# A last output stage by seven products, a finer start and a written-out order in an attention and MLP kernel

## The chip, the cores and the metric

One core of a Trainium2 chip. The metric is the device time of one execution in microseconds; lower is better. TensorE is called PE, VectorE DVE, ScalarE ACT, GpSimd POOL and SyncE SP, as in the profile. ACT and SP also issue transfers (queues ACTq and SPq).

## The reference

Causal attention for 4 batches, 12 heads, 448 positions and 64 dimensions per head, all float32, followed by an MLP with squared ReLU:

```python
scores = (q @ k.transpose(0, 1, 3, 2)) / np.sqrt(64)
scores = np.where(mask, -1e9, scores)            # mask: the columns behind the row
attn = softmax(scores)
x = (attn @ v).transpose(0, 2, 1, 3).reshape(1792, 768)
out = np.square(np.maximum(x @ w_in, 0)) @ w_out   # w_in 768 x 2048, w_out 2048 x 768
```

## The kernel before

Two heads make a pair, so there are 24 pairs (6 per batch). The first 12 pairs (batches 0 and 1) feed the first half of the tokens, the other 12 the second half.

**Attention** (`attention`, L341 to L550). A pair's q and k are brought to 64 dimensions x 448 positions per head. Either they are loaded in pieces of 128 bytes, eight transfers per pair (`load_qk`, L356), and transposed on DVE (`transposed`, L403), or they are loaded by rows, four transfers in pieces of 256 bytes (`load_rows`, L378), transposed on PE (`turned_rows`, L389) and copied out by ACT or DVE. `ROWS` says which pairs go by rows: 4 to 9. The scores of a pair (L422) come in seven chunks of 64 query rows; chunk c has 64(c+1) columns, as later columns are masked, so a head has 1792 columns in all. `PLACE` puts the chunks into four PSUM banks, and the first 12 pairs do chunks 6, 5, 0 in one group and 4, 3, 2, 1 in another. For each chunk DVE adds the mask and finds the row's extreme (L435, "mask pass" below), ACT takes the exponential with its sum (L439). When all seven sums are there, DVE forms the reciprocals (L515, L516), POOL or DVE normalises (L448), PE transposes the probabilities in four steps (L462), ACT or DVE copies them out (L318, L470) and PE multiplies by v (L482). Even and odd pairs have a set of buffers each, so the loads of pair 2 into the buffers of pair 0 wait until pair 0's q and k are transposed.

**Two terms.** x, the weights and the hidden values are split into a high and a low part, and a product is three instructions (high by high, high by low, low by high; "step" below), so as to keep float32's precision.

**First half of the tokens.** Plain products: `h_unit` (L679 to L681) and `o_unit` (L1098 to L1100), in four groups of 512 hidden columns.

**Second half of the tokens.** Here each stage is a product of 2 x 2 blocks done with seven block products in place of eight (Winograd's form of Strassen's scheme). `h_pair` makes the hidden values of a group for one of two halves u, `factor` splits them into seven left factors (11, 21, t2, t1, t3, 22, t4), `o_parts` makes the seven right factors from w_out, three loaded and four (s1 to s4) summed by `added_up` with adding transfers from POOL (L742) and copies (L752), and `o_seven` (L986 to L988) multiplies and adds. The groups come in the order `TURNS` = 0, 3, 2, 1. The last, group 1, is the exception: it takes the plain factors (11, 12, 21, 22 on both sides, all eight right factors loaded in two parts from `wo_split`), and `o_last` makes four result blocks with three column blocks d each, four steps x 3 instructions per half u pair, 144 in all. DVE adds each result to its sum (L321), transposes it (L1036), and four transfers of 56 KB store it (L1041). The very last one is stored in another way (`finish`): two halves, each transposed on PE (L1063), copied out and stored (L1078).

**The order.** Every operation is handed to `plan.op` with a rank, the engines that may do it and their costs. `Plan.emit` then runs a list schedule: with planned durations it picks the operation that can start first (by rank between equals), the engine and the buffer, and emits the instructions in the order of their planned starts. `AMENDS` shifts the ranks of stretches of operations. On the chip an engine works through its queue in that order. The order of stages is h of group 0 twice, then for each group the next group's h half 0, its own o stage, the next group's h half 1.

Of the kernel before, what the change touches and what calls it, by code (L numbers as in the profile page):

```python
# [20 lines left out]
class Op:  # L21
    __slots__ = ("rank", "ways", "then", "left", "ready", "take", "drop", "lag", "bias")
# [14 lines left out]
class Plan:  # L37

    LAG = {PE: 0.25, ACT: 0.3, DVE: 0.3, POOL: 0.3, DMA: 0.5, DMA2: 0.5}
    ISSUE = 1.4
    BEGIN, BACKLOG = 1.3, 2.5
    FEW = {PE: 0.0, ACT: 0.5, DVE: 1.0, POOL: 0.0, DMA: 0.0, DMA2: 0.0}
    MANY = {PE: 0.0, ACT: 0.0, DVE: 0.3, POOL: 0.0, DMA: 0.0, DMA2: 0.0}

    def __init__(self):  # L50
        self.ops, self.writer, self.readers = [], {}, {}
        self.pools, self.caps, self.held = {}, {}, {}
        self.bias = self.FEW

# [17 lines left out]
    def op(self, rank, ways, reads=(), writes=(), after=(), take=None, drop=(), clear=(), lag=0.0):  # L72
        o = Op()
        o.rank, o.ways, o.then, o.ready, o.take, o.drop = rank, ways, [], 0.0, take, drop
        o.lag, o.bias = lag, self.bias
# [18 lines left out]
        o.left = len(deps)  # L94
        for d in deps:
            d.then.append(o)
# [3 lines left out]
    def amend(self, table):  # L100
        for first, end, more in table:
            for o in self.ops[first:end]:
                o.rank += more

    def emit(self):
        free = [1.0, 1.9, 3.4, 2.7, 0.7, 0.7]
        ready = [o for o in self.ops if o.left == 0]
        order, port, net = [], 0.0, 0.0
        while ready:
            best = None  # L110
            for o in ready:
                at = o.ready + (self.ISSUE if o.ways[0][0] >= DMA else 0.0)
                if o.take:
                    h, n = o.take[0], len(o.take)
                    if self.held[h.kind] + n > self.caps[h.kind] or len(self.pools[h.pool]) < n:
                        continue
                    at = max(at, sorted(self.pools[h.pool])[n - 1][0])
                at += o.lag
                if o.ways[0][0] >= DMA:
                    at = max(at, net - self.BACKLOG)  # L120

                w = min(
                    (max(free[w[0]], at, port if shared(w) else 0.0) + w[1] + o.bias[w[0]],
# [4 lines left out]
                if best is None or key < best[0]:  # L128
                    best = (key, o, w)
# [61 lines left out]
def kernel(  # L191
# [21 lines left out]
    P = 128  # L213
# [1087 lines left out]
```

## Time and profile before

| | |
|---|---|
| median of 3 runs | 603.56 us (603.54 to 604.6) |
| profiled execution | 606.17 us, span 604.3 us |
| PE busy | 587.0 us, 3766 products and transposes |
| DVE, ACT, POOL busy | 418.8, 361.8, 348.1 us |
| DMA | 120.02 MB, mean 199 GB/s |
| mean granted TensorE clock | 0.999 |

The span runs from the first to the last instruction in the trace; the execution's own time has 1.87 us more around it. Products are pipelined: the duration of one reaches over the start of the next, so the cost of one in a row of many is the distance between two starts.

### The profile page before, as it was taken

What the parts mean: (1) busy time and instruction counts of PE and PEld (TensorE: products, weight loads), DVE (VectorE), ACT (ScalarE), POOL (GpSimd) and SP (SyncE); (2) the same over time, 40 slices, a digit from 0 to 9 for tenths busy, and PEclk for the clock granted to TensorE, in tenths of its full rate; (3) what the DMA queues carried; (4) which work ended last, traced back from release to release, by engine and by line L of the source; (5) the groups of instructions that cost most, each with busy time, mean ns of one, the idle gap of its engine ahead of it and who ended that gap; (6) DMA issues with size and microseconds to landing.
All of it is one profiled execution on the core that took longest, in us unless ns stands there. A gap on an engine that the chain in (4) does not pass through costs nothing.

```text
span 604.3 us, 11456 instructions
## 1 busy us (share of the span) xinstructions
PE 587.0 (97%) x3766; PEld 513.8 (85%) x3766; DVE 418.8 (69%) x951; ACT 361.8 (60%) x889; POOL 348.1 (58%) x460
## 2 busy tenths in 40 slices
PE   3999999999999999999999999999999999999997
PEld 2677777898988998888898889998999899999996
DVE  4997976366985887775677616688782777777454
ACT  3889997665687656577447543367764573752400
POOL 2574673764585844867557754256685566777000
PEclk9999999999999999999999999999999999999999
DMA  9899745979789888987898759869868746771555
GB/s 148 168 204 179 165 103 116 257 232 329 191 208 315 247 238 217 282 232 226 255 242 259 268 189 263 274 188 238 207 152 163 195 116 135 158 177 41 183 92 93
DMA packets 190652, 120.02 MB, mean 199 GB/s; under 512 B 126016, under 2 KB 178560, under 8 KB 190592
## 3 DMA queue, kind: packets, MB, share of 16 engines
q1 hardware_dynamic: 169488, 107.99, 64.8%
q0 software_dynamic: 6912, 9.44, 10.0%
q10 hardware_dynamic: 14192, 1.85, 1.9%
q8 instruction: 30, 0.49, 0.3%
q14 instruction: 30, 0.25, 0.2%
HBM read 80.71 MB, written 38.54 MB: 197 GB/s over the span
## 4 chain that ended last, share of the span: by engine, by line
PE 90%; DMA 4%; ACT 2%; SPq 2%; issue 1%; DVE 0%; ACTq 0%; DVEq 0%
PE ps L1098 7%; PE ps L679 7%; PE ps L1100 6%; PE ps L1099 6%; PE ps L681 6%; PE ps L680 6%; PE ps L482 6%; PE ps L462 6%; PE ps L986 6%; PE ps L988 6%; PE ps L987 6%; PE ps L422 5%; PE ps L860 5%; PE ps L864 5%; PE ps L862 5%; DMA words<-in_moe_w_in_dram 2%
## 5 line engine op out<-in xcount | busy, mean ns | idle before, releaser
L318 ACT ACTIVATE words<-words 128x384 f32<-128x384 f32 (+3 forms) x140 | 79.8, 597 | 27.9 <-DVE words L321 15.3
L448 POOL TENSOR_SCALAR ap<-ap,asm 128x64 f32<-128x64 f32 (+6 forms) x123 | 74.6, 626 | 30.6 <-DVE asm L516 27.7
L435 DVE CUSTOM_DVE_ANT_0 ps<-ps,mask 128x448 f32<-128x448 f32 (+6 forms) x168 | 68.4, 446 | 19.2 <-PE ps L422 12.9
L1098 PE MATMUL ps<-wo,g 128*128 128x384 f32 x224 | 76.8, 343 | 0.0
L1100 PE MATMUL ps<-wo,g 128*128 128x384 f32 x224 | 75.1, 335 | 0.0
L1099 PE MATMUL ps<-wo,g 128*128 128x384 f32 x224 | 75.0, 335 | 0.0
L679 PE MATMUL ps<-x,wi 128*128 128x448 f32 x192 | 74.1, 386 | 0.6 <-ACT aqt L318 0.6
L681 PE MATMUL ps<-x,wi 128*128 128x448 f32 x192 | 70.3, 366 | 0.0
L680 PE MATMUL ps<-x,wi 128*128 128x448 f32 x192 | 70.3, 366 | 0.0
L439 ACT ACTIVATE ap<-ps,mx 128x448 f32<-128x448 f32 (+6 forms) x126 | 59.2, 487 | 15.0 <-DVE mx L435 11.1
L325 POOL TENSOR_TENSOR wi<-words,wi 128x384 fp32r<-128x384 f32 (+1 forms) x44 | 52.6, 1204 | 11.8 <-ACT wi L318 6.6
L860 PE MATMUL ps<-x,wi 128*128 128x448 f32 x156 | 57.3, 367 | 0.3 <-DMA wi<-wi_split 0.3
L318 ACT ACTIVATE r<-ps 128x448 f32<-128x448 f32 x60 | 32.5, 545 | 41.4 <-PE ps L681 17.5
L862 PE MATMUL ps<-x,wi 128*128 128x448 f32 x156 | 57.2, 367 | 0.0
L864 PE MATMUL ps<-x,wi 128*128 128x448 f32 x156 | 57.2, 367 | 0.0
L986 PE MATMUL ps<-g,wi 128*128 128x448 f32 x153 | 56.0, 366 | 0.3 <-DMA wi<-wo_split 0.3
L987 PE MATMUL ps<-g,wi 128*128 128x448 f32 x153 | 56.0, 366 | 0.0
L988 PE MATMUL ps<-g,wi 128*128 128x448 f32 x153 | 56.0, 366 | 0.0
L331 POOL TENSOR_SCALAR wi<-words 128x384 fp32r<-128x384 f32 (+1 forms) x39 | 26.9, 689 | 46.6 <-DVE words L643 23.0
L640 DVE TENSOR_SCALAR words<-words 128x384 int32<-128x384 int32 (+1 forms) x56 | 30.3, 543 | 23.2 <-ACT words L318 23.1
L321 DVE CUSTOM_DVE_ANT_0 words<-words 128x768 uint16<-128x768 uint16 (+1 forms) x56 | 42.3, 755 | 5.8 <-ACT words L318 3.3
L318 ACT ACTIVATE apt<-ps 128x512 f32<-128x512 f32 x65 | 35.6, 611 | 14.5 <-PE ps L462 14.4
(149 smaller groups left out, 1459.9 us busy)
## 6 DMA issues: line engine op xcount, KB each, us to landing
words<-in_moe_w_in_dram SPq DMA_DIRECT2D x24, 512.0 KB, 5.6
words<-in_moe_w_out_dram SPq DMA_DIRECT2D x32, 384.0 KB, 3.7
wo_split<-wo SPq DMA_DIRECT2D x26, 384.0 KB, 4.8
wi<-wo_split SPq DMA_DIRECT2D x24, 384.0 KB, 4.1
wo_whole<-words SPq DMA_DIRECT2D x32, 192.0 KB, 3.9
wi_split<-wi SPq DMA_DIRECT2D x24, 256.0 KB, 4.0
v<-in_v_dram SPq DMA_DIRECT2D x24, 192.0 KB, 4.1
wi_whole<-words SPq DMA_DIRECT2D x18, 256.0 KB, 4.0
```

What stands on the lines that cost most here:

```text
L318: return (ACT, t_act(n, psum, more), lambda: nc.scalar.activation(dst(), src(), func, **kw))
L679: nc.tensor.matmul(o, w[:, 0], x[:, 0], start=c == 0, stop=False)
L680: nc.tensor.matmul(o, w[:, 0], x[:, 1], start=False, stop=False)
L681: nc.tensor.matmul(o, w[:, 1], x[:, 0], start=False, stop=c == NP - 1)
L860: nc.tensor.matmul(o, w.t[:, 0, c], x[:, 0], start=begin and c == 0, stop=False, skip_group_check=True)
L862: nc.tensor.matmul(o, w.t[:, 0, c], x[:, 1], start=False, stop=False, skip_group_check=True)
L986: nc.tensor.matmul(o, w.t[:, 0, d], g.t[:, 0], start=start, stop=False, skip_group_check=True)
L987: nc.tensor.matmul(o, w.t[:, 0, d], g.t[:, 1], start=False, stop=False, skip_group_check=True)
L988: nc.tensor.matmul(o, w.t[:, 1, d], g.t[:, 0], start=False, stop=stop, skip_group_check=True)
L1098: nc.tensor.matmul(res(), g[:, 0], w[:, 0], start=f == 0, stop=False)
L1099: nc.tensor.matmul(res(), g[:, 0], w[:, 1], start=False, stop=False)
L1100: nc.tensor.matmul(res(), g[:, 1], w[:, 0], start=False, stop=f == GF - 1)
```

## The change

- **Last o stage.** Group 1 also has seven factors on either side. `o_last` loops over the three column blocks and, in each, over the seven products (`O_LAST`); results that share a partial sum share a bank, and after each product DVE adds the bank to one of the sums. That is 126 products. Four right factors per half u are now summed (`added_up`), six are loaded. Both h halves of group 1 now precede the o stage of group 2. The tiles of x are lent as buffers for factors once their last product is done (`lent_x`).
- **Rows.** `ROWS` is 4 to 7; pairs 8 and 9 are loaded in 128-byte pieces and transposed on DVE.
- **First two pairs.** Pair 0 has its chunks in six banks (`SOON`) and three groups of scores; pair 1 has two new groups (`NEXT`). Reciprocals and normalising are done for chunks 0 to 4 and for 5 and 6 apart.
- **Products of zeros.** A tile of x is cleared by DVE first; ten products of 448 columns with it stand ahead of pair 0's scores, four times three behind them.
- **Order.** `emit` makes no schedule any more: a table gives each operation its place; the place divided by three orders them, the remainder names the engine.

```diff
+    SOON = {6: (0, 0), 5: (1, 0), 4: (2, 0), 3: (3, 0), 1: (4, 0), 2: (5, 0), 0: (5, 3 * QC)}
+    NEXT = {**PLACE, 0: (3, 7 * QC)}
+    FAST = 2
-    ROWS, RB = range(4, 10), S // NK
+    ROWS, RB = range(4, 8), S // NK
...
+    zero = x_t[-1][:, 0]
+    nc.vector.memset(zero.bitcast(F32), 0.0)
...
+    WARM = (10, (3, 3, 3, 3))
+    def warmed(rank, n, after):
+        ps = Hold("ps", "mm")
+        def go():
+            for i in range(n):
+                nc.tensor.matmul(ps.t[:, :S], zero[:, :P], zero, start=True, stop=True)
...
+        if fast:
+            groups = ((6, 5), (4, 3, 2, 1, 0)) if n else ((4, 3), (2, 1, 0), (6, 5))
+        if n == 0:
+            warmed(at - 20, WARM[0], ())
         for chunks in groups:
             softmax(chunks, at)
             at += 2.0
...
+        if n == 0:
+            for m in WARM[1]:
+                warmed(at + 100, m, started[:3])
+        for first, end in ((0, 5), (5, NQ))[::-1 if n else 1] if fast else ((0, NQ),):
+            def inverse(sums=s.sm[:, first:end]):
...
+    O_LAST = {"11": ("a", "11"), "12": ("b", "11"), "s2": ("a", "12"), "s1": ("c", "22"),
+              "s3": ("a", "22"), "s4": ("c", "12"), "22": ("a", "21")}
...
-            if gr != TURNS[-1]:
-                added_up(rank, CH, source, done, lambda t: t, True)
+            added_up(rank, CH, source, done, lambda t: t, True)
...
-        for k in ("11", "21", "12", "22"):
-            i, j = k
-            for d in range(CB):
-                ps, a = Hold("ps", "os"), o_sum(k, d)
-                rank = o_product(ps, [(W[i + m, u], g7[TURNS[-1], m + j, u]) for m in "12" for u in range(2)],
-                                 d, True, True, rank, step)
+        bank = {}
+        for d in range(CB):
+            for key, (b, k) in O_LAST.items():
+                begin = key in ("11", "12", "s1")
+                if begin:
+                    bank[b] = Hold("ps", "os")
+                ps, a = bank[b], o_sum(k, d)
+                rank = o_product(ps, [(W[key, u], g7[TURNS[-1], OTHER[key], u]) for u in range(2)],
+                                 d, begin, True, rank, step)
+                if (key, d) == ("22", CB - 1):
+                    finish(ps, k, d, rank)
                     continue
...
+                if key in ("12", "22", "s3", "s4"):
+                    put_out(k, d, rank)
...
-        stages += [(a, 0) for a in after] + [(gr, None)] + [(a, 1) for a in after]
+        early_pair = after == TURNS[-1:]
+        stages += [(a, 0) for a in after] + [(a, 1) for a in after if early_pair]
+        stages += [(gr, None)] + [(a, 1) for a in after if not early_pair]
...
+    def emit(self, table):
+        codes = [int(x, 36) for x in table.split()]
...
+        for n, (code, o) in enumerate(sorted(zip(codes, self.ops), key=lambda x: x[0])):
...
+            o.ways[code % 3][2]()
```

Read against the order in which the operations are made, the table has 3508 places and says for the start: on PE the ten zero products, pair 0's scores in groups (2, 1, 0), (6, 5), (4, 3), three zero products, pair 1's scores (4, 3, 2, 1, 0), (6, 5), six zero products, pair 0's probabilities' first transposes, three zero products, the other transposes, pair 2's scores; on DVE pair 0's k and q transposed, its mask passes 1, 2, 0, 6, 3, 4, pair 1's q and k transposed, pass 5, reciprocals, one normalising, reciprocals, pair 1's passes; on SP pair 0's k, half of pair 1's k, one load of pair 2's k, the rest of pair 1's k, loads of pair 2, the first weights, and only then v. For the end: the last 47 steps on PE are 42 of the last stage and 5 of the one before, mixed; the last column block comes as 11, 12, s1, s2, s4, s3, 22, with the stores of the sums of s4 and s3 ahead of the finish.

## Rows read from the trace of the kernel before

**Rows 1.** The page: busy us of each engine (share of the span), instructions.

```profile
PE 587.0 (97%) x3766; PEld 513.8 (85%) x3766; DVE 418.8 (69%) x951; ACT 361.8 (60%) x889; POOL 348.1 (58%) x460
```

**Rows 2.** The page: the chain that ended last, by engine.

```profile
PE 90%; DMA 4%; ACT 2%; SPq 2%; issue 1%; DVE 0%; ACTq 0%; DVEq 0%
```

**Rows 3.** Windows: stretch, length, busy us by engine (instructions), clock, DMA share, GB/s.

```profile
30.00:60.00 30.00, 28.98 (x282) 21.70 (x283) 25.45 (x82) 28.18 (x88) 18.60 (x32) 1.00 0.99 193
60.00:100.00 40.00, 40.00 (x374) 29.66 (x374) 33.04 (x113) 34.63 (x108) 26.03 (x48) 1.00 0.61 140
```

**Rows 4.** Windows from the first product on, cut where TensorE settles.

```profile
6.73:32.76 26.03, 20.77 (x199) 14.23 (x199) 21.25 (x75) 19.46 (x64) 12.37 (x23) 1.00 0.91 172
32.76:599.30 566.54, 565.53 (x3565) 499.17 (x3563) 394.54 (x863) 341.22 (x825) 333.38 (x426) 1.00 0.77 202
```

**Rows 5.** Waits of TensorE: us in total, times, longest.

```profile
PE ps L422 <- DVE aqt L403: 7.3, 2, 6.7
PE ps L422 <- DVE asm L515: 3.2, 1, 3.2
```

**Rows 6.** Timeline of TensorE, scores of pairs 0, 1, 2: start, us.

```profile
6.73 3.27 PE L422 MATMUL ps<-akt,aqt 64*64 64x448 f32 x28 [6.73 <-DVE aqt L403]
13.22 3.10 PE L422 MATMUL ps<-bkt,bqt 64*64 64x320 f32 x28 [3.22 <-DVE asm L515]
...
18.85 1.75 PE L422 MATMUL ps<-akt,aqt 64*64 64x320 f32 x28 [0.61 <-DVE aqt L403]
```

**Rows 7.** Groups by form on TensorE, at 6 to 12 and 18.5 to 20.7 us.

```profile
L422 PE MATMUL ps<-akt,aqt 64*64 64x448 f32 x4 | 1.8, 978 | 6.7 <-DVE aqt L403 6.7
...
L422 PE MATMUL ps<-akt,aqt 64*64 64x448 f32 x4 | 0.9, 536 | 0.0
```

**Rows 8.** Windows: the last o stage's products.

```profile
569.94:599.29 29.35, 29.35 (x145) 26.86 (x143) 15.99 (x26) 2.54 (x5) 0.00 (x0) 1.00 0.52 90
```

**Rows 9.** Groups of DVE from 569.9 us on, of POOL at 500 to 570 us.

```profile
L321 DVE TENSOR_TENSOR sb<-ps,sb 128x448 f32<-128x448 f32 (+2 forms) x13 | 7.5, 585 | 12.9 <-PE ps L988 12.9
L1036 DVE STREAM_TRANSPOSE words<-sb 128x448 f32<-128x448 f32 x10 | 6.4, 644 | 0.3
...
L325 POOL TENSOR_TENSOR w<-words,w 128x384 fp32r<-128x384 f32 x2 | 2.0, 1016 | 0.1
```

**Rows 10.** Timeline of TensorE: four transposes of rows and the next product.

```profile
38.94 0.55 PE L389 MATMUL ps<-ident,rows 112*128 112x112 f32 x4
39.26 0.45 PE L679 MATMUL ps<-x,wi 128*128 128x448 f32 x1
```

**Rows 11.** DMA queues at 2 to 14 and 20 to 60 us.

```profile
DMA packets 13427, 1.97 MB, mean 164 GB/s; under 512 B 13427, under 2 KB 13427, under 8 KB 13427
...
DMA packets 22928, 7.53 MB, mean 188 GB/s; under 512 B 22281, under 2 KB 22281, under 8 KB 22921
```

**Rows 12.** Timeline: loads of pair 1, mask passes, transposes.

```profile
6.41 0.86 SPq L356 DMA_DIRECT2D bk<-in_k_dram  x2
...
8.64 0.63 DVE L435 CUSTOM_DVE_ANT_0 ps<-ps,mask 128x448 f32<-128x448 f32 x1 [1.89 <-PE ps L422]
...
12.00 0.64 DVE L403 STREAM_TRANSPOSE bkt<-bk 128x448 f32<-128x448 f32 x1
...
15.07 0.50 DVE L435 CUSTOM_DVE_ANT_0 ps<-ps,mask 128x320 f32<-128x320 f32 x1 [1.00 <-PE ps L422]
```

**Rows 13.** Line L356 at 0 to 15 us: 128-byte loads.

```profile
DMA to landing us min/median/max: 2.3/3.0/5.2
```

**Rows 14.** Timeline of the end on SP.

```profile
600.87 0.98 SPq L1078 DMA_DIRECT2D out_dram<-words  x2
```

**Rows 15.** DMA issues: tile, queue, count, KB each, median us to landing.

```profile
words<-wo_whole SPq DMA_DIRECT2D x12, 192.0 KB, 3.6
```

**Rows 16.** Lines L742 (adding transfers) and L752 (copies): us or ns min, median, max.

```profile
DMA to landing us min/median/max: 3.4/5.5/8.3
...
L752 POOL TENSOR_SCALAR words<-words x5: 502/807/882, 450.5 to 512.4; 128x384 f32<-128x384 f32 x5
```

More of the change, by code (lines that the diff above doesn't have):

```diff
@@ L21 @@
 class Op:
-    __slots__ = ("rank", "ways", "then", "left", "ready", "take", "drop", "lag", "bias")
+    __slots__ = ("rank", "ways", "take", "drop", "deps")
 class Hold:
@@ L73, in op @@
         o = Op()
-        o.rank, o.ways, o.then, o.ready, o.take, o.drop = rank, ways, [], 0.0, take, drop
-        o.lag, o.bias = lag, self.bias
+        o.rank, o.ways, o.drop = rank, ways, drop
         o.take = () if take is None else take if isinstance(take, tuple) else (take,)
@@ L93, in op @@
                 self.readers.setdefault(k, []).append(o)
[L94 to L96 removed]
+        o.deps = deps
         self.ops.append(o)
         return o
[L100 to L123, printed above, removed]
[L124 to L138 removed]
+    def emit(self, table):
+        codes = [int(x, 36) for x in table.split()]
+        assert len(codes) == len(self.ops)
+        done = set()
+        for n, (code, o) in enumerate(sorted(zip(codes, self.ops), key=lambda x: x[0])):
+            assert all(d in done for d in o.deps)
             for h in o.take:
@@ L142, in emit @@
                 h.tile = entry[1:]
-                self.held[h.kind] += 1
+            o.ways[code % 3][2]()
             for h in o.drop:
                 h.drops -= 1
-                h.free = max(h.free, end + self.LAG[e])
                 if h.drops == 0:
-                    self.pools[h.pool].append((h.free,) + h.tile)
-                    self.held[h.kind] -= 1
-            for t in o.then:
-                same = all(x[0] == e for x in t.ways) and e < DMA
-                t.ready = max(t.ready, end + (0.0 if same else self.LAG[e]))
-                t.left -= 1
-                if t.left == 0:
-                    ready.append(t)
-        assert len(order) == len(self.ops)
-        order.sort(key=lambda x: x[:2])
-        for _, _, o, i in order:
-            o.ways[i][2]()
-        return max(free)
+                    self.pools[h.pool].append((n + 1,) + h.tile)
+            done.add(o)
 def t_mm(n, m=128):
@@ L898, in h_pair @@
         square("11")
-        factor("11", "11", plain)
+        factor("11", "11", False)
         product("s3", "d", True)
@@ new lines, in o_last, with put_out, go @@
+        return rank
+    def put_out(k, d, rank):
+        i, j = k
+        a, h = o_sum(k, d), Hold("f", "tr")
+        plan.op(rank, [(DVE, t_dve(S) + 0.05, lambda: nc.vector.transpose(h.t, a()))],
+                [("sum", k, d)], [h], take=h)
+        row, col = T + (int(j) - 1) * S, (int(i) - 1) * CH + d * P
+        for s in range(P // SQ):
+            def go(eng, s=s):
+                return lambda: eng.dma_start(
+                    out=out[row:row + S, col + s * SQ:col + (s + 1) * SQ].rearrange(
+                        "(b p) d -> p b d", p=SQ),
+                    in_=h.t[s * SQ:(s + 1) * SQ].rearrange("p (b d) -> p b d", d=SQ))
+            plan.op(rank, [(DMA, 0.6, go(nc.sync), t_dma(S, 128)), (DMA2, 0.6, go(nc.scalar), t_dma(S, 128))], [h], [], drop=[h])
```

250 lines of the change are left out of this document (176 added, 74 removed), and 48 rows, old and new, of the table AMENDS.

## The prediction

> **What bounds the kernel now.** The page's busy line comes first: TensorE is busy for 587.0 of 604.3 us [rows 1], and the chain of work that ended last runs over TensorE for 90% [rows 2]. A busy TensorE says nothing of how much of its work is needed, so the next view is the span in stretches. At 30 to 60 us TensorE works for 28.98 us, at 60 to 100 us without a gap [rows 3]. Cut at the point where it settles, the view says it more sharply: between its first product at 6.73 us and 32.76 us it is busy for 20.77 of 26.03 us; from there to 599.30 us it idles for only 566.54 - 565.53 = 1.0 us [rows 4]. So from 33 us on the time is the sum of TensorE's instructions, and only fewer of them help there; ahead of 33 us it is the chain through VectorE (DVE), ScalarE (ACT) and the loads; behind 599.3 us it is a tail of 5.0 us.
>
> The waits at the start are 6.7 us for the first transposed q and k (in a sum of 7.3) and 3.2 us in the middle of it [rows 5]. The timeline shows a second loss: the 28 score products of a pair take 3.27 us for pair 0, 3.10 for pair 1 and 1.75 for pair 2 [rows 6], and the widest form took 978 ns at 6 to 12 us against 536 ns later [rows 7]. The granted clock reads 1.00 (2.4 GHz) in every stretch, but a factor of 1.8 in one form is what 1.2 GHz would give, so I take the first two pairs to have run at 1.2 GHz; ahead of pair 0 TensorE had done nothing, ahead of pair 1 it had idled for 3.2 us.
>
> **Seven products in the last stage.** Before, four results times three column blocks times four factors times three terms are 144 products; after, seven times three times two times three are 126. Each lasts 365 ns in the list of groups, but they overlap: 144 of them (the count of the row has one neighbour more) fill 29.35 us, 0.204 us each [rows 8]. **18 fewer are -3.67 us**, and all of it lies on the path, since TensorE has no gap there. The price is paid on other engines. VectorE adds 20 whole results instead of 11 and still transposes 11: 20 x 0.59 + 11 x 0.64 = 18.8 us, with the finish about 20, beside 126 x 0.204 = 25.7 us of products [rows 9], so it stays hidden as long as the seven banks let it lag. GpSimd gets sums and splits of the weights, 8 adding transfers and 8 low parts of 1.02 us [rows 9]; it stood idle in this stage [rows 8]. Three more factors per half column, and the differences they come from, have to be ready before the stage ends. The change therefore puts both h halves of the last group ahead of the o stage of the group before, so that stage's 25.7 us of products cover them. I cost these at nothing; the cover ends where the first rival begins.
>
> **Rows for four pairs.** Pairs 8 and 9 lose 16 transposes on TensorE. Four of them move the next product back by 39.26 - 38.94 = 0.32 us [rows 10], so **16 are -1.28 us**, between nothing (if TensorE waits there instead) and twice that, if their weight loads hold up their neighbours. The four copies out of PSUM become four transposes on VectorE, no dearer. In their place SP issues sixteen transfers of 128-byte pieces instead of eight of 256-byte pieces. The DMA engines are 0.99 busy at 30 to 60 us and 0.61 at 60 to 100 us [rows 3]; 128-byte pieces alone moved at 164 GB/s, the mix at 20 to 60 us at 188 GB/s [rows 11]. For 16 x 56 KB that is 0.9 MB / 164 - 0.9 MB / 188 = 0.7 us of DMA time, hidden if the weights of the first group, loaded on the same queue, are not late. The Trainium skill (DMA: Bandwidth & Descriptors, Specifications) wants at least 512 bytes in a piece for full rate, which speaks against this part; by it both forms are slow, and the sum would lose the 1.28 us if the loads of 30 to 60 us decided. No run here separates the two forms yet.
>
> **The start.** The first product can't come sooner: it waits for pair 0's transposed q until 6.73 us [rows 6], and the loads ahead of that are the same. What changes is behind it. (a) The first group of scores is chunks 2, 1, 0, 384 of a head's 1792 columns, instead of 6, 5, 0 with 896. At pair 2's rate that is 0.38 us, at pair 0's rate 0.70; the 896 took 1.64 us, and the first mask pass followed 0.27 us later, at 8.64 us [rows 6, 12]. So VectorE begins at 7.4 us (7.7 at the slow rate) instead of 8.64. (b) Pair 0 has its chunks in six banks, so no pass waits for an exponential in the same bank; its passes took 8.64 to 12.00 us with gaps, and without them VectorE reaches pair 1's transposes before 10 us. (c) There it meets the loads: the last two of pair 1's k stand on SP behind one load for pair 2, which waits for pair 0's k to be transposed (about 6.1 us). They are issued at about 6.7 to 7.6 us; before it was 6.41 us, also for two [rows 12]; with the 3.0 us that such a load took [rows 13], pair 1's transposes end at about 11.2 us. (d) Scores of its first five chunks at the full rate take 0.94 us, and its first pass starts at 11.2 + 0.94 + 0.27 = 12.4 us instead of 15.07 [rows 12]. That is 2.7 us; a normalising pass and a second pair of reciprocals have moved to VectorE, pair 2's transposes have moved behind: 0.4 us off. **I take -2.3 us**, carried to 33 us, since VectorE and ACT are the bound there. Both ends: nothing, if ACT alone sets the pace by 33 us, and -5.3 - 2.8 = -8.1 us, if no wait and no slow product were left [rows 4, 6].
>
> The ten products of zeros start once VectorE has cleared a tile, and last 10 x 0.41 = 4.1 us at the slow rate (twice 0.204): over ahead of 6.73 us if they start by 2.6 us, and late by what they start later. The other twelve are 2.4 us in places where TensorE waited before (3.2 us ahead of pair 1, then for the normalised chunks), so they cost nothing if that wait stays, at most 1.2 us between pair 1's scores and the first transposes of probabilities.
>
> The Trainium skill (TensorE: Matmul & The Clock Gate, Part 1) says that the half rate is the default and that activity ends it, at a point that varies between runs; the two rates agree with [rows 6, 7]. By it the zeros should bring pair 0's scores to full rate in most runs, not in all.
>
> **The order** is a table now. At run time an engine still executes its queue in order, so only a different order can cost or gain. Of the 1.0 us of gaps left after 33 us [rows 4] it can win that much; what it can lose I bound by twice that: -1.0 to +2. I take nothing, the middle of what stands there now.
>
> **The tail.** The last two blocks but one are now stored within the last 2.5 us of products, eight transfers of 56 KB, ahead of the final stores on the same two queues. Before, one such block left just ahead. From last product to the final issue it was 600.87 - 599.3 = 1.6 us [rows 14]. I take +0.3 us, between 0 and 1.5 (three issues of 0.49 us on SP, as in that row).
>
> **Sum.** -3.67 - 1.28 - 2.3 + 0.3 = -6.95 us. The profiled execution took 606.17 us with a span of 604.3, so 599.2; the median of the runs is 2.6 us below the profiled one, so **596.6 us**.
>
> **Rivals.**
> Slow scores stay: the zeros don't lift the clock by 6.7 us, or it falls in the gap. Then pair 0's last pass ends at about 11.1 us, pair 1's first pass comes at about 14.3, and 0.75 instead of 2.3 us is won: 598.1 us. For it speaks that pair 1 was slow 3.2 us after 3.3 us of work [rows 6].
> More is won: VectorE's shorter start also closes the later waits, -5 instead of -2.3: 593.9 us. Against it, VectorE and ACT have little room until 33 us.
> New waits inside: the small pieces delay the first group's weights, or a reordered queue stops TensorE. Nothing from the rows, nothing from the start's surplus and +2 of gaps: 600 to 603 us.
> The slower side: the summed weights of the last stage are late. For its second half column a load, three adding transfers in a row with a copy ahead of each, and a split have to end before the first product with s4 there. With 3.6 us for the load [rows 15], 5.5 us per adding transfer, 0.8 per copy [rows 16] and 2 x 1.02 us for the split [rows 9] that is 24.5 us; in the table 50 product steps, 50 x 0.61 = 30.6 us, lie between. It decides from 7.5 us per transfer on; the slowest took 8.3 [rows 16], which would cost 2.3 us. To end over 1.2 us slower than before it takes a stall of 6.95 + 1.2 = 8.2 us, 5.5 + (6.1 + 8.2) / 3 = 10.3 us per transfer: about 605 us.
>
> **Chances.** The forecast 0.53, slow scores 0.17, more won 0.11, new waits 0.13, the slower side 0.06. A measurement of this kernel can tell about 0.2%, 1.2 us, from no change. The first three are faster; of the new waits 0.04 ends within 1.2 us of 603.56. So 0.89 faster, 0.05 same, 0.06 slower. The range 593.2 to 600.4 us holds the forecast with its bounds, the slow scores, most of the larger gain and the mild end of the new waits, about 0.8.
>
> **What would show it.** 126 products in the last stage at 0.204 us; 32 transposes of rows instead of 48; ten zero products ending before 6.7 us and score products of the widest form near 540 ns in pair 0; pair 1's first mask pass near 12.4 us; TensorE without gaps from about 30 us; last product to end within 5.5 us. The prediction is wrong if gaps of over 2 us stand behind 33 us, above all ahead of the last stage's s4 products, or if pair 1's first pass is not before 14 us.

## The result and the profile after

| | before | after |
|---|---|---|
| median of 6 runs | 604.21 us (603.54 to 605.28) | 610.80 us (608.62 to 612.44) |
| profiled execution, span | 606.17 us, 604.3 us | 610.65 us, 608.8 us |
| first score product to the end of the last o product | 6.73 to 599.3 us | 6.88 to 603.8 us |
| behind the last product | 5.0 us | 5.0 us |

The changed kernel takes 1.0108 times as long (95% interval 1.0087 to 1.0129): 6.6 us more, where 7 us less were forecast. Two executions of e6 below (1494 and 2049 us) and one of e11 (612.6 us) were slow ones and are left out of the ratios.

The page's busy line of the kernel after, against [rows 1]:

```profile
PE 591.8 (97%) x3754; PEld 515.5 (85%) x3754; DVE 472.5 (78%) x1083; ACT 356.6 (59%) x886; POOL 302.9 (50%) x395
```

TensorE has 12 instructions fewer (18 products and 16 transposes less, 22 zeros more) and is yet busy for 4.8 us longer (the zeros alone take 7.4 us of its time); VectorE has 54 us more work, GpSimd 45 us less. The windows, cut as in [rows 4], then two stretches of 25 and 50 us:

```profile
6.88:32.76 25.88, 22.58 (x212) 15.41 (x213) 21.16 (x81) 19.94 (x64) 9.52 (x19) 1.00 0.84 170
32.76:603.84 571.08, 564.29 (x3531) 496.52 (x3529) 447.96 (x987) 335.61 (x822) 291.06 (x365) 1.00 0.78 202
...
350.00:375.00 25.00, 23.20 (x115) 22.01 (x114) 19.63 (x25) 9.81 (x19) 11.54 (x13) 0.93 0.73 223
...
550.00:600.00 50.00, 47.98 (x233) 43.09 (x232) 45.58 (x72) 14.82 (x31) 30.01 (x31) 1.00 0.70 148
```

Read the first two numbers of a line against each other. Behind 32.76 us TensorE now idles for 571.08 - 564.29 = 6.8 us; before it was 1.0. In the last 50 us VectorE is busy for 45.6. Before, roughly the same part of the work (either stretch ends about 4 us ahead of the last product's end) looked like this:

```profile
550.00:595.00 45.00, 45.00 (x223) 41.64 (x223) 24.24 (x41) 8.82 (x16) 8.92 (x9) 1.00 0.49 114
```

So VectorE went from 54% to 91% there, GpSimd from 20% to 60%. Gaps are only a part: an instruction whose neighbour waits is also recorded longer. I therefore took the distance from each TensorE start to the next, subtracted the median distance of the same pair of forms behind 33 us in the kernel before, and summed the differences ("lost", in us; zeros ahead of 6.8 us are left out, the later ones count as lost, 2.8 of the 14.1 us in the first row):

| stretch | before | after | experiment e10 (below) |
|---|---|---|---|
| up to 33 us | 13.7 | 14.1 | 14.2 |
| 33 to 350 | 37.7 | 41.0 | 40.9 |
| 350 to 375 | 1.1 | 3.7 | 0.0 |
| 375 to 550 | 1.5 | 1.4 | 0.6 |
| behind 550 | 0.5 | 4.6 | 1.8 |
| work by the medians | 539.0 | 533.1 | 533.0 |

The work fell by 5.9 us: the products and transposes taken out did save what they cost. Lost time rose by 0.4 + 3.3 + 2.6 - 0.1 + 4.1 = 10.3 us. The sum of both, 4.4 us, is the difference of the spans, 4.5. The waits of TensorE name who was late:

```profile
PE ps L1082 <- DVE g L272: 1.8, 1, 1.8
PE ps L957 <- DVE sa L272: 1.5, 1, 1.5
...
PE ps L957 <- DVE sb L272: 1.3, 2, 0.7
PE ps L386 <- DVE bkt L364: 1.2, 1, 1.2
PE ps L446 <- DVE bpt L434: 1.0, 1, 1.0
```

All are for VectorE. By the timeline they end at 364, 555, 573 and 602, 12 and 27 us: many small places, no single large one. The largest, in the timeline of all engines:

```profile
359.99 4.19 DVE L272 TENSOR_TENSOR g<-r,g 128x448 fp32r<-128x448 f32 x1 [2.35 <-ACT g L269]
360.16 1.43 POOL L276 TENSOR_TENSOR g<-r,g 128x448 fp32r<-128x448 f32 x1
361.29 3.32 POOL L282 TENSOR_SCALAR x<-words 128x448 fp32r<-128x448 f32 x5
...
364.23 0.44 PE L1082 MATMUL ps<-wo,g 128*128 128x384 f32 x1 [1.80 <-DVE g L272]
...
365.53 0.61 DVE L272 TENSOR_TENSOR g<-r,g 128x448 fp32r<-128x448 f32 x1
```

The first and the last line are the same operation on two tiles: 0.61 us alone, 4.19 us beside a row of GpSimd instructions, one of two tiles and five copies. It ends about as the row ends (364.2 and 364.6 us), and the low part of g that it makes is what the product at 364.23 waits for. Then the clock falls (granted 0.93 on the mean of 350 to 375 us, in the window above), and that stretch loses 2.6 us more than before for a wait of 1.8.

The wait that ends at 555 us has the same picture ahead of it:

```profile
550.72 2.96 DVE L272 TENSOR_TENSOR f<-f,r 128x448 f32<-128x448 f32 x1
...
550.88 1.34 POOL L276 TENSOR_TENSOR x<-words,x 128x384 fp32r<-128x384 f32 x1
551.86 1.33 POOL L276 TENSOR_TENSOR wi<-words,wi 128x384 fp32r<-128x384 f32 x1
...
554.80 0.47 PE L957 MATMUL ps<-g,w 128*128 128x448 f32 x1 [1.45 <-DVE sa L272]
```

The sum that the product waits for stands behind that add in VectorE's queue.

The start, on TensorE (rows of scores, probabilities by v, the first h product), and on VectorE pair 1's first mask pass:

```profile
6.88 3.27 PE L386 MATMUL ps<-akt,aqt 64*64 64x192 f32 x28 [1.38 <-DVE aqt L364]
...
12.27 1.75 PE L386 MATMUL ps<-bkt,bqt 64*64 64x320 f32 x28 [1.24 <-DVE bkt L364]
...
18.61 1.75 PE L386 MATMUL ps<-akt,aqt 64*64 64x448 f32 x28
...
27.09 1.20 PE L446 MATMUL ps<-bpt,v 128*64 128x320 f32 x12 [1.03 <-DVE bpt L434]
...
30.51 0.45 PE L651 MATMUL ps<-x,wi 128*128 128x448 f32 x1
```

```profile
13.75 0.41 DVE L399 CUSTOM_DVE_ANT_0 ps<-ps,mask 128x256 f32<-128x256 f32 x1
```

Against [rows 6, 12]: pair 1's scores run at the full rate and its first pass comes at 13.75 instead of 15.07 us, so 1.3 us were won. At pair 2's scores, 18.61 against 18.85, 0.2 is left, and the first h product comes at 30.51 where it came at 30.20. The windows show what holds it:

```profile
16.00:20.00 4.00, 3.60 (x39) 2.38 (x41) 3.72 (x17) 4.00 (x14) 1.88 (x5) 1.00 0.96 161
```

ACT is busy for all of the 4 us, VectorE for 3.72; before it was 3.78 and 3.58 us.

### The profile page after: what moved, and what is told of

Same layout as the page of the kernel before. It is cut to its first block, busy times and chain, and to the rows that moved or that the text cites. A ratio compares the mean times of both kernels' runs of the same rounds, so it can differ in the third digit from the quotient of the medians.

```text
span 608.8 us, 11469 instructions
## 1 busy us (share of the span) xinstructions
PE 591.8 (97%) x3754; PEld 515.5 (85%) x3754; DVE 472.5 (78%) x1083; ACT 356.6 (59%) x886; POOL 302.9 (50%) x395
## 4 chain that ended last, share of the span: by engine, by line
PE 81%; DVE 6%; ACT 4%; DMA 4%; SPq 2%; issue 2%; POOL 0%; DVEq 0%; ACTq 0%; POOLq 0%
PE ps L1080 6%; PE ps L1082 6%; PE ps L1081 6%; PE ps L651 6%; PE ps L653 6%; PE ps L652 6%; PE ps L446 5%; PE ps L836 5%; PE ps L834 5%; PE ps L832 5%; PE ps L957 5%; PE ps L426 5%; PE ps L959 5%; PE ps L958 5%; PE ps L386 4%
## 5 line engine op out<-in xcount | busy, mean ns | idle before, releaser
L399 DVE CUSTOM_DVE_ANT_0 ps<-ps,mask 128x384 f32<-128x384 f32 (+6 forms) x168 | 68.2, 443 | 24.9 <-PE ps L386 12.7
L403 ACT ACTIVATE ap<-ps,mx 128x320 f32<-128x320 f32 (+6 forms) x126 | 59.2, 479 | 26.3 <-DVE mx L399 25.1
L651 PE MATMUL ps<-x,wi 128*128 128x448 f32 x192 | 73.5, 383 | 0.0
L653 PE MATMUL ps<-x,wi 128*128 128x448 f32 x192 | 70.3, 366 | 0.0
L652 PE MATMUL ps<-x,wi 128*128 128x448 f32 x192 | 70.2, 366 | 0.0
L412 POOL TENSOR_SCALAR ap<-ap,asm 128x448 f32<-128x448 f32 (+6 forms) x76 | 44.1, 597 | 44.5 <-DVE asm L488 24.6
L834 PE MATMUL ps<-x,wi 128*128 128x448 f32 x147 | 53.9, 367 | 0.0
L836 PE MATMUL ps<-x,wi 128*128 128x448 f32 x147 | 53.9, 366 | 0.0
L832 PE MATMUL ps<-x,wi 128*128 128x448 f32 x147 | 53.8, 366 | 0.0
L272 DVE TENSOR_TENSOR g<-r,g 128x448 fp32r<-128x448 f32 x50 | 42.0, 846 | 11.1 <-ACT g L269 11.1
L269 ACT ACTIVATE r<-ps 128x448 f32<-128x448 f32 x55 | 29.8, 543 | 34.1 <-PE ps L836 17.6
L282 POOL TENSOR_SCALAR wi<-words 128x384 fp32r<-128x384 f32 (+1 forms) x33 | 21.4, 648 | 53.0 <-DVE words L615 36.7
L1082 PEld LDWEIGHTS ps<-wo,g 128*128 128x128 f32 x224 | 42.6, 190 | 2.1 <-DVE g L272 2.1
L1080 PEld LDWEIGHTS ps<-wo,g 128*128 128x128 f32 x224 | 42.6, 190 | 0.7
L269 ACT ACTIVATE wi<-words 128x384 fp32r<-128x384 f32 (+1 forms) x52 | 27.8, 539 | 25.7 <-DVE words L272 11.5
L1081 PEld LDWEIGHTS ps<-wo,g 128*128 128x128 f32 x224 | 42.5, 190 | 0.3
L426 PE MATMUL ps<-ident,ap 128*128 128x128 f32 x288 | 40.0, 274 | 0.9 <-ACT bp L403 0.5
```

The lines of the kernel that those rows point to most:

```text
L269: return (ACT, t_act(n, psum, more), lambda: nc.scalar.activation(dst(), src(), func, **kw))
L399: plan.op(at, [(DVE, t_dve(w), lambda: nc.vector.tensor_tensor_reduce(out=at_(), in0=at_(), in1=mask[:, S - w:], scale=-SCALE, scalar=3.0e ...
L426: nc.tensor.transpose(ps.t[:, n * P:(n + 1) * P], s.p[:, POFF[c] + kc * P:POFF[c] + (kc + 1) * P], ident[:, o:o + P])
L651: nc.tensor.matmul(o, w[:, 0], x[:, 0], start=c == 0, stop=False)
L652: nc.tensor.matmul(o, w[:, 0], x[:, 1], start=False, stop=False)
L653: nc.tensor.matmul(o, w[:, 1], x[:, 0], start=False, stop=c == NP - 1)
```

## The experiments

Two theories stood from the start. **Order:** the operations are worth what was forecast, but the table puts some of them so that VectorE or a buffer is late. **Operations:** the finer work itself (more for VectorE and GpSimd in the last stage, small loads, zeros) costs more than it saves in any order. Medians are given with the ratio to the kernel before and its 95% interval.

**e1, the later twelve products of zeros left out.**

```diff
-    WARM = (10, (3, 3, 3, 3))
+    WARM = (10, ())
```

> The changed kernel with the ten products of zeros ahead of pair 0's scores, and without the twelve later ones. Theory (the later zeros stand where TensorE has nothing else to do, and they keep pair 1's scores at the full rate): pair 1's scores take 3 us and more instead of 1.75, the first H product starts at 30.5 to 32 us (30.51 with them), 611 to 612 us. Rival (the zeros delay what is queued behind them by most of the 4.2 us they take): the first H product starts before 29 us, 608 to 609 us.

Measured: 611.37 us, 1.0098 (1.0068 to 1.0128), first h product 30.86 us. Scores of pairs 0 and 1:

```profile
6.83 1.74 PE L386 MATMUL ps<-akt,aqt 64*64 64x192 f32 x28 [1.76 <-DVE aqt L364]
...
11.59 3.23 PE L386 MATMUL ps<-bkt,bqt 64*64 64x320 f32 x28 [3.03 <-DVE bkt L364]
```

Without the later zeros pair 1's scores stand behind a gap of 3.03 us and take 3.23 us (half rate), in after they take 1.75. That the zeros make this difference is not shown: in e1 pair 0's scores ran at the full rate and ended earlier, and in e3, e10 and e12, where they did so too, pair 1's scores took 2.39, 2.52 and 3.26 us with the later zeros in place (last section). It is worth nothing in time, as pair 2's scores begin at 18.6 us (after) and 18.7 (e1).

**e2, five of GpSimd's copies to ACT.** The high parts of five left factors, of the row at 361 us (the edit in words; it changes five codes of the table).

```diff
- xpart 11 (0, 1, 2), 21 (1), t3 (0), high part: GpSimd
+ xpart 11 (0, 1, 2), 21 (1), t3 (0), high part: ACT
```

> The changed kernel with the five copies x<-words that POOL makes back to back at 361 us put on ACT; nothing else moves. Theory (the VectorE add of 4.19 us at 360 us is held back by POOL's work beside it): that add takes 0.6 to 1.5 us, TensorE's wait of 1.8 us at 362 and the fall of the clock behind it go, the clock of 350 to 400 us is 1.00, 607 to 608 us. Rival (the add is long for a reason of its own, or the wait passes to ACT, which gets 3 us more there): a wait of over 1 us stays between 358 and 370 us, 610 to 611.5 us.

Measured: 608.31 us, 1.0066 (1.0041 to 1.0091); span 606.3 against 608.8. The add at that place, and the waits that stand now:

```profile
360.96 2.27 DVE L272 TENSOR_TENSOR g<-r,g 128x448 fp32r<-128x448 f32 x1 [2.48 <-ACT g L269]
```

```profile
PE ps L957 <- DVE sa L272: 1.5, 1, 1.5
PE ps L957 <- DMA w<-wo_split: 1.3, 1, 1.3
```

The add falls from 4.19 to 2.27 us (one GpSimd instruction beside it instead of six), not to the 0.6 to 1.5 expected, and no product waits for it. The row of copies was the cause of that wait; 0.2 us are lost in 362 to 375 us where 3.7 were. In time it is 2.5 us by the medians; the intervals of the two ratios just touch (up to 1.0091, and from 1.0087 in after).

**e3, the transposes of the last stage left out.**

```diff
-        plan.op(rank, [(DVE, t_dve(S) + 0.05, lambda: nc.vector.transpose(h.t, a()))],
+        plan.op(rank, [(DVE, t_dve(S) + 0.05, lambda: None)],
...
-                    in_=h.t[s * SQ:(s + 1) * SQ].rearrange("p (b d) -> p b d", d=SQ))
+                    in_=a()[s * SQ:(s + 1) * SQ].rearrange("p (b d) -> p b d", d=SQ))
```

> The changed kernel with the eleven VectorE transposes of the last o stage left out: the output's blocks of that stage are stored as they lie in the sums, untransposed, except the last one. VectorE loses 11 x 0.64 = 7 us between 568 and 603 us. Theory (VectorE, busy over 90% from 550 to 590 us, is what TensorE waits for in the last stage): TensorE's waits from 568 us on, about 2.3 us, go, the last product ends at 601 to 602 us instead of 603.8, 608 to 609 us; the 1.5 us of wait at 553 us stays, since it lies ahead of the first transpose. Rival (the waits come from the summed weights or from the order, not from how much VectorE has to do): the waits stay, 610 to 611 us.

Measured: 610.19 us, 1.0095 (1.0066 to 1.0123). Between 550 and 590 us nothing is lost any more (2.9 us in after). But the edit can't have done that: in after 2.6 of the 2.9 us are lost ahead of 574 us, at the waits that end at 555 and 573, and the first of the transposes left out stands at 578.0 us. Behind 574 us, where they stand, the loss fell only from 2.1 to 1.8 us. So this run does not show the transposes to be the cause of the gaps, which was my theory. What changed at the first place is the timing: VectorE comes to the add of 2.96 us 3.4 us later than in after, GpSimd to its sums 4.3 us later, so that the sums begin when the add is done, and it takes 0.93:

```profile
554.12 0.93 DVE L272 TENSOR_TENSOR f<-f,r 128x448 f32<-128x448 f32 x1
...
555.13 1.33 POOL L276 TENSOR_TENSOR x<-words,x 128x384 fp32r<-128x384 f32 x1
```

The time did not follow either: the same table lost it earlier in this execution. A wait for a load, and the window behind it:

```profile
PE ps L957 <- DMA w<-wo_split: 1.9, 1, 1.9
```

```profile
440.00:450.00 10.00, 10.00 (x44) 9.05 (x43) 4.31 (x5) 5.49 (x12) 6.25 (x8) 0.86 0.69 136
```

The load was issued at 433.6 us, when the last product that reads its buffer was done, and landed at 439.0; the mean clock of the next 10 us was 0.86.

**e4, the changed operations with a list schedule.** The scheduler of the kernel before, without corrections of ranks.

```diff
-    plan.emit(PLACES)
+    plan.emit()
```

> The operations of the changed kernel, all of them, in the order that the list scheduler of the kernel before gives them, without its table of corrections. Theory (the 18 products and 16 transposes saved are worth 5 us of TensorE's time whatever the order, and the order of the table gives 6 us back in collisions and in a VectorE that is late at the end): the waits move to other places; 603 to 612 us, and no add of VectorE over 3 us. Rival (the table is the better order, and the loss lies in the operations themselves): 613 us and more, with the same busy VectorE and waits at 550 to 605 us.

Measured: 620.72 us, 1.0247 (1.0216 to 1.0278), the longest wait 4.7 us for a sum of VectorE, behind an add of two tiles of 6.56 us. My range missed, and the time lies in that of the rival (the operations themselves); this run can't separate the two, e10 does. The table is 10 us better than an order that nobody fitted.

**e5, the kernel before with the last stage by seven products alone**, its scheduler and corrections kept for every operation that both have.

```diff
+    O_LAST = {"11": ("a", "11"), "12": ("b", "11"), "s2": ("a", "12"), "s1": ("c", "22"),
+              "s3": ("a", "22"), "s4": ("c", "12"), "22": ("a", "21")}
...
+        early_pair = after == TURNS[-1:]
```

> The kernel before, with its scheduler and its corrections (each kept with its operation), and of the change the last o stage alone: seven products, and all that comes with it (the extra factors, the summed weights of that stage, the second H pair drawn ahead). If the 18 products count as the prediction has them (3.67 us, with VectorE and POOL covered): 600 to 601 us. Theory (VectorE and the weights of the last stages come late, in any order): busy VectorE over 85% and TensorE's waits of 2 to 5 us behind 540 us, 602 to 606 us.

Measured: 616.50 us, 1.0198 (1.0173 to 1.0223), far above what either theory gave. TensorE's waits, then VectorE and GpSimd in the timeline:

```profile
PE ps L990 <- DVE sb L326: 9.6, 3, 7.0
```

```profile
570.71 8.69 DVE L326 TENSOR_TENSOR g<-f,g 128x448 fp32r<-128x448 f32 x1
...
573.35 3.54 POOL L330 TENSOR_TENSOR x<-words,x 128x384 fp32r<-128x384 f32 x3
```

GpSimd runs seven sums and low parts from 571.4 to 578.9 us, one behind the other (three of them in the line shown), and one add of VectorE, which had 1.00 us just before, stays open for 8.69 us. Everything behind it in VectorE's queue is late, and TensorE stands for 7.0 us.

**e6, the kernel before with rows for four pairs alone; e7, with the finer start alone.**

```diff
-    ROWS, RB = range(4, 10), S // NK
+    ROWS, RB = range(4, 8), S // NK
```

```diff
+            warmed(at - 20, WARM[0], ())
...
+        for first, end in ((0, 5), (5, NQ))[::-1 if n else 1] if fast else ((0, NQ),):
```

> The kernel before with its scheduler and corrections, and of the change the rows alone: pairs 8 and 9 load q and k by VectorE's transposes again. By the prediction (16 TensorE transposes fewer, 1.28 us, the four VectorE transposes covered): 602 to 603.5 us. Rival (the smaller pieces of these loads, or VectorE, hold up pairs 8 and 9): waits of 1 us and more between 45 and 150 us that the kernel before has not, 604 to 608 us.

> The kernel before with its scheduler and corrections, and of the change the start alone: finer first two pairs and the products of zeros. By the prediction (pair 1's first mask pass at 12.4 us, a lead of 2.3 us that lasts): first H product at 28 us, 601.3 to 602.5 us. Theory (the zeros don't lift the clock for pair 0, and the lead of a microsecond at pair 1 is gone again by 30 us): first H product at 29.5 to 31 us, 603 to 606 us.

Measured: e6 609.01 (profiled) and 614.66 us, 1.0130 (1.0071 to 1.0189); e7 612.90 us, 1.0148 (1.0127 to 1.0168), its first h product at 31.14 us, 0.9 us later than before. Neither tells the price of its part. Every operation that changes shifts the schedule behind it: e6 has a new wait of 2.0 us for ACT, which ends at 48 us; e7's new waits of 2.4 and 1.6 us end at 431 and 446 us, some 400 us behind the edit. What follows is only how brittle an order is.

**e8, all operations of the change in the order of the old scheduler with its corrections.**

> All operations of the change in the order of the scheduler of before with its corrections, each kept with its operation (new operations have none). If the order of the table is what costs: 597 to 603 us, with TensorE's waits behind 33 us under 4 us in sum. If the operations themselves cost it, or any order that was not fitted to them: 606 to 616 us, with new waits of 1 us and more in several places.

Measured: 624.19 us, 1.0328 (1.0305 to 1.0351), above both ranges. The same picture as in e5, on other tiles:

```profile
PE ps L1017 <- DVE sb L332: 7.5, 2, 7.2
```

```profile
580.64 1.31 POOL L336 TENSOR_TENSOR x<-f,x 128x384 fp32r<-128x384 f32 x1
580.68 6.61 DVE L332 TENSOR_TENSOR sb<-sb,sa 128x448 f32<-128x448 f32 x1
...
587.75 0.61 DVE L332 TENSOR_TENSOR sb<-sb,sa 128x448 f32<-128x448 f32 x1
```

So the operations without a fitted order are 20 us slower than before; the table wins 13 of them back, not all.

**e9 and e10, the table mended.** No operation is touched; e2's five copies stay on ACT. e9 moves 22 operations against e2 (in words, as for e10 to e12):

```diff
+ VectorE before 555 us: a low part of group 2 17 places earlier; a sum and a squared ReLU of group 1 a few places apart
+ TensorE at 88 to 110 us: two h products of group 0 earlier, as fill; turns of pair 11's probabilities later
+ TensorE, ACT at 434 to 438 us: two products of block 12 and their sums later, so that the weight load is in
+ end: the last column block with s3 ahead of s4, with the sums, transposes and stores behind them
```

> The changed kernel with the five copies on ACT, and with twenty-four places of the table moved, nothing added or left out. At 548 us VectorE's add g<-r,g goes ahead of POOL's row of work and the two sums that TensorE waits for go ahead of the next add of two tiles; at 434 us the product whose weights come late goes behind three that have theirs; at 88 to 110 us two H products go ahead of the scores and two ahead of the turns that wait for VectorE; at the end the last block's s4 products go between its s3 and 22 products, which use one bank. Theory (the loss is a sum of such places, each the price of an order that no engine can leave): the waits of 1.5 us at 551, 1.3 at 434, 0.9 at 110 and 0.7 at 599 us go or halve, 603.5 to 605.5 us against 608.3. Rival (VectorE and POOL together are full in these stretches, so a wait that goes at one place comes at the next): TensorE's waits behind 33 us stay within 1 us of what they were, 607 to 609 us.

Measured: 609.44 us, 1.0104 (1.0059 to 1.0149). The wait at 555 us was gone: the add of VectorE that stood ahead of it (3.13 us in e2, beside GpSimd's sums) now came before them and took 0.62. The last product ended at 600.1 us (603.8 in after, 601.3 in e2), but the tail behind it grew from 5.0 to 6.9 us (two stores stood ahead of ACT's last copy), and two waits had only moved: 1.1 us at 440 us, now for ACT, and 1.3 us at 111 us, where I had moved the products of the wrong pair. e10 corrects these three:

```diff
- e9's later turns of pair 11
+ TensorE: one h product ahead of pair 12's turns; VectorE: one normalising of pair 12 earlier
+ ACT: the sum of block 11 (d 1) 17 places earlier
+ end: s1 and s2 exchanged too; stores exchanged together with their queues
```

> As the run before, with its two misplaced steps mended. The last block's products alternate between two banks (s2, s1, s3, s4, 22), and its stores keep the queues that the places had, so that ACT has one store, not two, ahead of the last copy. At 438 us ACT's copy of the sum that TensorE waited for goes ahead of two others. At 109 us VectorE's last normalise goes ahead of the add, and one H product ahead of the turns that wait for it. Theory (the loss is a sum of places): the tail is 3.7 us again (5.6 in the run before), the waits of 1.2 us at 438 and 1.5 at 109 go, the last product ends at 597 to 599 us, 602 to 604 us. Rival (waits only move): the last product ends at 601 us or later, 605 us and more.

Measured: 603.71 us, 0.9996 (0.9979 to 1.0013), 7 us less than after. Windows and waits:

```profile
32.76:597.59 564.83, 562.52 (x3535) 495.22 (x3533) 442.90 (x991) 336.58 (x827) 285.07 (x360) 1.00 0.79 204
...
350.00:400.00 50.00, 50.00 (x271) 48.27 (x271) 31.67 (x50) 20.02 (x40) 26.52 (x27) 1.00 0.81 249
```

```profile
PE ps L386 <- DVE bkt L364: 2.2, 1, 2.2
...
PE ps L446 <- DVE bpt L434: 1.0, 1, 1.0
...
PE ps L1045 <- DVE sb L272: 0.5, 1, 0.5
```

The gaps behind 32.76 us fell from 6.8 to 2.3 us; the last product ends at 596.3 us, and 597.59 is the end of the final transposes behind it. The long waits that are left stand in the start. The order theory holds as far as the loss goes: 26 operations moved and seven given to another engine, among 3508, carry the whole difference between after and before. That these operations can gain what was forecast in some order is not shown.

**e11, e10 with the five copies back on GpSimd.**

```diff
- the five high parts: ACT
+ the five high parts: GpSimd
```

> The run before with one thing put back: the five copies x<-words at 361 us on POOL, as the change has them. Theory (VectorE's add of two tiles gets no turn while POOL's instructions follow one another): an add of over 3 us at 360 us, a TensorE wait of 1.5 to 3 us at 362 and a lower clock behind it, 606 to 608 us, 2.5 to 3.5 us over the run before. Rival (ACT's copies only moved other things, and the gain of the second experiment was scatter): 603 to 604.5 us.

Measured: 605.33 us, 1.0026 (1.0004 to 1.0048). The add, the copies, and the product's wait:

```profile
359.54 3.12 DVE L272 TENSOR_TENSOR g<-r,g 128x448 fp32r<-128x448 f32 x1 [2.49 <-ACT g L269]
359.77 3.32 POOL L282 TENSOR_SCALAR x<-words 128x448 fp32r<-128x448 f32 x5
```

```profile
PE ps L1082 <- DVE g L272: 0.7, 1, 0.7
```

The same add in e10, where no product waited for it:

```profile
359.75 1.64 DVE L272 TENSOR_TENSOR g<-r,g 128x448 fp32r<-128x448 f32 x1 [2.45 <-ACT g L269]
```

The blocked add and its wait are back (3.12 us, 0.7 us), so the mechanism is right. Its size is not 2.5 to 3.5 us: the medians differ by 1.6 us, the intervals of the two ratios overlap a little (up to 1.0013 and from 1.0004), and the profiled executions, 602.94 us here and 603.40 in e10, stand the other way round. The wait is 0.7 us where after had 1.8: most of the block is covered here.

**e12, e10 with another order at 25 us and 102 us.**

```diff
+ VectorE: the copy of pair 1's second group of turned probabilities, and those turns, ahead of pair 3's k
+ TensorE: one h product ahead of the turns at 102 us
```

> The mended kernel with two more places moved: one H product more goes ahead of the turns at 102 us (a wait of 0.9 us), and VectorE copies pair 1's last turned probabilities and transposes pair 3's k ahead of the first word pieces (TensorE waits 1.2 us for that copy at 25.5 us). Theory (the start is bound by ACT and VectorE together, ACT being busy all the time from 16 to 20 us): the wait at 102 goes, the wait at 25.5 goes but comes again as a wait for the first H weights or the next turns, first H product not before 30 us, 602.5 to 603.5 us. Rival (the start was lost at that copy alone): first H product at 29.3 us, 601.5 to 602.3 us.

Measured: 604.01 us, 1.0015 (0.9992 to 1.0038). The wait did not go, it moved to pair 3's scores:

```profile
28.86 1.75 PE L386 MATMUL ps<-bkt,bqt 64*64 64x448 f32 x28 [1.42 <-DVE bqt L364]
```

The first h product starts at 30.91 us, against 30.52 in e10: moving a copy of VectorE ahead only made its next work late. That place was as expected, the time 0.5 us above it. No version ran faster than the kernel before.

## Why the prediction was wrong

**Seven products, the count: right.** 126 products at the rate of before, and together with the rows 5.9 us less work on TensorE by the medians, where 3.67 + 1.28 = 4.95 were forecast. The two are not separated.

**Seven products, "I cost these at nothing": wrong, one of the two steps that failed.** VectorE's own 20 us beside 25.7 us of products were counted right: taking the transposes away gains 0.3 us behind 574 us (e3). Not counted was what comes just ahead of them: the sums of the group before and of the second h half that was drawn there, and GpSimd's sums of weights. VectorE is busy for 45.6 of the 50 us from 550 on, and its adds of two tiles grow when GpSimd works beside them. Lost time behind 550 us rose by 4.1 us, 2.6 of it ahead of 574 us, and e9 took the largest wait there away by moving an add ahead of GpSimd's row. So at that wait the cover failed by VectorE and GpSimd meeting; that the one at 573 us has the same cause is not shown.

**The order at nothing, "what it can lose I bound by twice that: -1.0 to +2": wrong, and the larger failure.** The 1.0 us of gaps of the old order says what is left to win, and nothing of what another order can lose. The new operations have to be fitted into queues whose order was made for others; orders that nobody fitted gave 616 to 624 us (e4, e5, e8). In the table itself the losses behind 33 us rose by 9.9 us, and its gaps of 6.8 us there met the prediction's own sign of being wrong. 3.3 of the 9.9 us lie at 33 to 350 us and stay in e10; the other 6.6 lie behind, and e10 took 7 us of the time back by moves and changes of engine alone. That is the rival "new waits inside", whose price of 2 us was five times too small.

**The start, "-2.3, carried to 33 us": wrong in its second half.** Steps (a) to (d) came as ordered: pair 1's scores at the full rate and the first pass at 13.75 us, 1.3 us earlier and within the point that I had set (14 us), though not at 12.4. Part of that miss is pair 0, whose scores were still at half rate in the profiled execution (3.27 us); in e10, with pair 0 at the full rate, the first pass came at 13.07 us. The lead was gone at 18.6 us. I had named the reason ("VectorE and ACT are the bound there") and drawn the opposite from it: in a stretch that these two fill the lead of TensorE was not passed on, and of the first pass's 1.3 us 0.2 were left at pair 2's scores. Nor was it the slow pair 0: the first h product came at 30.51 us with it (after) and at 30.52 to 30.91 us with a fast one (e1, e3, e10, e12). The term came out at its lower bound, nothing; lost time up to 33 us even rose by 0.4.

**The zeros "cost nothing":** no cost was found (e1: 611.37 us without the later ones, 610.80 with them). They brought pair 0's scores to the full rate in four of eight profiled executions of the table, not in most. **The tail +0.3:** it stayed at 5.0 us, so nothing.

**The slower side, late summed weights: not what happened.** No product of the last stage waited for s4 in after; the waits for weights in e2 and e3 stood at 434 to 439 us, for a loaded factor of another stage. The time came out on that rival's side, slower than before, through the order and not through it.

**Rows:** sixteen transposes fewer are in the 5.9 us. Of the small pieces no price was found: 33 to 350 us lose 3.3 us more than before, in after and in e10 alike, and whether the loads, the moved transposes on VectorE or the order does this stays open, as e6 has other waits of its own. The prediction's 164 GB/s for 128-byte pieces alone is a misreading: the 1.97 MB in 13427 packets [rows 11] are 147 bytes each on the mean, with loads of v among them. It was not tried to fit an order to the seven products with the start and the rows of before.

**What e10 leaves open.** It saves 6.0 us of TensorE's work by the medians, loses 0.5, 3.2 and 1.3 us more than before up to 33, from 33 to 350 and behind 550 us, and 2.0 less between. Its profile is 2.8 us shorter than that of before, the median only equal to it; the profiled execution of before was 2 us above its median, so nothing is to be concluded from the two profiles alone.

## What to carry to other kernels

Where TensorE has no gaps, removing products saves exactly their time only if the queues of the other engines are fitted anew: price the order as a term of its own, by a schedule that nobody fitted, not by the gaps that are left. Look for stretches in which the added work of VectorE and GpSimd meets, and bound an add of two tiles there by the length of GpSimd's whole row and not by its own 0.6 us. Such a meeting hangs on timing (2.96 us in after, 0.93 in e3 for the same add), so credit an edit with a loss that vanished only where the edit acts. A lead ahead of a stretch that other engines fill was worth nothing behind it here.

## What the hardware did that I had not expected

**An add of VectorE that gets no turn.** An add of two tiles in SBUF took 0.61 us alone, 2.27 beside one GpSimd instruction (e2), 2.96 beside two (after, at 551 us), 3.12 beside five copies in a row (e11), 4.19 beside six (after), 6.61 beside six (e8) and 8.69 beside seven (e5), and ended about with the row (within 0.5 us). The Trainium skill (SBUF — State Buffer, SBUF: two separate sides) says that VectorE, with two inputs in SBUF, and GpSimd share a pair of ports, and that the one that starts first has it for its whole instruction while the other blocks. The traces agree that VectorE blocks; but the block lasted here over a whole row of instructions, not over one, as if GpSimd took the ports again each time before VectorE did. And by the recorded starts VectorE was the first at 550.72 and at 359.99 us (GpSimd at 550.88 and 360.16) and was blocked all the same; as spans on GpSimd are rough, the traces do not settle who comes first.

**Zeros lift the rate in some executions only.** The same ten products of zeros (from 1.40 us on) stood ahead of pair 0's scores in every run of the table. The 28 score products then took, in us:

| | after | e2 | e9 | e11 | e3 | e10 | e12 | e1 (no later zeros) |
|---|---|---|---|---|---|---|---|---|
| pair 0 | 3.27 | 3.26 | 2.69 | 2.56 | 1.74 | 1.74 | 1.74 | 1.74 |
| pair 1 | 1.75 | 1.75 | 1.75 | 1.75 | 2.39 | 2.52 | 3.26 | 3.23 |

Where pair 0 was slow, it ended late, TensorE idled for 0.7 to 1.2 us ahead of pair 1, and pair 1 was fast. Where pair 0 was fast, the gap was 2.2 us (3.0 in e1) and pair 1 was slow in part or wholly. So the rate was only moved from one pair to the other, and the later zeros did not hold it. For pair 1 in e12 the granted clock says the same, 0.50:

```profile
11.62 3.26 PE L386 MATMUL ps<-bkt,bqt 64*64 64x320 f32 x28 [2.24 <-DVE bkt L364]
```

```profile
11.60:14.80 3.20, 3.18 (x28) 1.72 (x28) 2.35 (x11) 0.90 (x5) 1.84 (x4) 0.50 0.95 220
```

For pair 0 in after, and for both pairs before, it reads 1.00 beside half the rate: the trace's records of the clock begin only at 10.3 us in after and at 16.0 us before, and ahead of the first record the column shows 1.00. There the durations have to be read. A gap of 1.8 us at 362 us did lower the column, to 0.93 on the mean of 25 us.

**Spread.** Runs of after lie between 608.6 and 612.4 us, those of e10 between 602.9 and 608.8, those of before in the first comparison between 603.5 and 605.3, but in that of e1 to e4 between 603.4 and 608.0. Whether an order written out by hand spreads more is not shown.
